# A rebuilt loading phase in a fused attention and gated feed-forward kernel on one Trainium2 core: what is loaded first, from which queue, and in what order two batches are worked through

## The chip, the cores and the metric

The kernel runs on one core of a Trainium2 chip. The metric is the time of one execution in device microseconds (us): 227.48 us, the median of three runs (227.17 to 228.03). A difference of under about 0.5% (1.14 us) can't be told from no change. The engines are named as in the profile: PE is the matmul engine (TensorE), PEld its weight loads, DVE is VectorE, ACT is ScalarE, POOL is GpSimd, SP is SyncE. SPq, POOLq and ACTq are the same engines where they issue DMAs. Each engine works through its instructions strictly in the order in which the program gives them.

## The reference

`x` is (8 batches, 8 heads, 512 tokens, 64) and `state` is (8, 8, 32, 64), both float32. Per batch and head:

```python
scores  = x @ state.T / 8            # 512 x 32
xread   = softmax(scores) @ state    # 512 x 64, the tokens read the state
scores2 = state @ x.T / 8            # 32 x 512
sread   = softmax(scores2) @ x       # 32 x 64, the state reads the tokens
attn    = concat([xread, sread])     # 544 rows per batch, heads side by side: 512 columns
# then, over all 8 * 544 = 4352 rows
out = (sigmoid(attn @ w_gate) * (attn @ w_val)) @ w_out   # 512 -> 1536 -> 512
```

## The kernel before, in words

**Tiling.** Matmul operands are bf16, sums are float32 in PSUM. For the tokens the kernel never forms `xread`: it multiplies the state with the weights first (`SW` = state times `w_gate` and `w_val`, per batch and head) and then the softmax weights `a` with `SW`. So per batch `b` the steps are, by the names of the helpers (line numbers are those of the profile):

- `load_x` (L78) brings x of a batch, 1 MB of float32, into `xf`; `cast_x` (L103) makes `xb` in bf16 from some of its heads; `xT` is its transpose, either with PE (`xT_mm` L118, copied out by `xT_cp` L123) or with four DMA transposes on SP (`at_xT_dma`, L128).
- `S_mm` (L134) makes the scores from `xT` and the zero-padded state `sTz`, `S_exp` (L139) their exponentials `E`. `n_sum` (L152, L154) sums and inverts on DVE, `n_mul` (L186) normalizes to `ab`, and `aT` is its transpose, by PE (`aT_mm` L193, `aT_cp` L203) or by DMA (`aT_dma`, L207).
- `sw_visit` and `sw_wide` make columns of `SW` from the transposed state `sTc` and the weights `wg`, `wv` (`sw_mm`, L249); `sw_cp` (L287) copies each result out of PSUM, on ACT or DVE. `sw_visit(b, lo, n, w)` needs columns lo to lo+n of weight w (0 is gate, 1 is value; without w both).
- `gv_mm` (L301) makes 128 of the 1536 hidden columns for gate and value (four 128x512 matmuls), `gv_th` (L311, ACT) a tanh in place of the sigmoid, `gv_glu` (L316, DVE) the product. `out_mm` (L332) multiplies four of twelve hidden blocks with `wo`; every third call finishes 128 rows, scales them on ACT (L336) and stores them (L338).
- `at_Eb` (L145), `p_tok` (L167 to L172), `sr_mm` (L223, L226), `sr_inv`, `sr_fin` (L231, L239) form `sread` for the state rows, which go through the feed-forward stage at the very end (L304, L352).

**Order.** The schedule is manual: the order of calls is the order of each engine's instructions. Up to the end of the `gv` work of batches 0 and 1 it is a list of calls written out by hand; after it a loop over b = 1 to 8 takes `out_mm` of batch b-1 and `gv_mm` of batch b in turn, and prepares batch b+1.

**Loads.** Weights are float32 in HBM and cast by the DMA, issued from POOL (`load_w` L83, `load_wo` L97). In the list before, SP issues the whole state `sf` (512 KB, L369), x of batch 0 in two halves and x of batch 1. POOL issues the weights one piece at a time, and between them it executes `gate` (L87): a one-element copy of something that must have landed or of a tile that is free, which holds back what POOL issues next. x of batch 1 is held by a small `memset` on POOL (`hold`, L74). The order on POOL is value columns 0 to 255, gate 0 to 255, gate 256 to 511, value 256 to 511, gate 512 to 1023, value 512 to 1023, gate 1024 to 1535, value 1024 to 1535, x of batch 2, the three thirds of `wo`, then (after the transposes of x of batch 2) x of batch 3. `pad` (L402) fills `sTz` from `sTc` on POOL; `pad(2, 6)` does batches 2 to 7.

**Warming.** `warm(n)` (L366) runs n matmuls whose result nobody reads, to keep PE busy; 80 of them before the real work.

**PSUM.** Pools named GV (2 buffers), SWP (4), OU (1) and AT (1) hold the results; a place is free again when its copy is done.

## Time and profile before

| what | value |
|---|---|
| runs: median, lowest, highest | 227.48, 227.17, 228.03 us |
| profiled execution: first to last instruction (span) | 226.7 us, granted PE clock 1.000 |
| busy PE / PEld / DVE / ACT / POOL over the span | 217.3 / 112.6 / 140.0 / 130.5 / 48.6 us |
| PE busy in 0 to 5, 5 to 10, 10 to 15, 15 to 20 us | 3.64, 3.92, 2.97, 4.97 us |
| PE busy in 20 to 40, 40 to 45, 45 to 65 us | 20.00, 4.43, 19.65 us |
| DVE and ACT busy in 15 to 45 us | 27.01 and 23.40 us |
| DMA share in 0 to 5, 5 to 10, then each 5 us to 45 | 0.64, 1.04, 1.35, 1.26, 1.13, 1.12, 1.20, 1.41, 1.19 |
| read from HBM, written to HBM | 18.35 MB, 8.91 MB |

The median is about 0.8 us above the profiled span: what lies before the first and after the last instruction, and the scatter of the runs. Busy matmul time counts pipelined matmuls, so a busy PE isn't PE at its peak. The DMA share is a mean over the core's 16 DMA engines; it passes 1 where packets of several transfers are open at once. An issue's "us to landing" runs from the issue to the last byte's arrival, so it holds the time in the queue too.

### The profile page before, as it was taken

What the parts mean: (1) busy time and instruction counts of PE and PEld (TensorE: products, weight loads), DVE (VectorE), ACT (ScalarE), POOL (GpSimd) and SP (SyncE); (2) the same over time, 40 slices, a digit from 0 to 9 for tenths busy, and PEclk for the clock granted to TensorE, in tenths of its full rate; (3) what the DMA queues carried; (4) which work ended last, traced back from release to release, by engine and by line L of the source; (5) the groups of instructions that cost most, each with busy time, mean ns of one, the idle gap of its engine ahead of it and who ended that gap; (6) DMA issues with size and microseconds to landing.
All of it is one profiled execution on the core that took longest, in us unless ns stands there. A gap on an engine that the chain in (4) does not pass through costs nothing.

```text
span 226.7 us, 4784 instructions
## 1 busy us (share of the span) xinstructions
PE 217.3 (96%) x1851; PEld 112.6 (50%) x1876; DVE 140.0 (62%) x233; ACT 130.5 (58%) x244; POOL 48.6 (21%) x96
## 2 busy tenths in 40 slices
PE   7869999999999999999999999999999999999994
PEld 7755344444444544444544444454445444466744
DVE  2579899866458855886488648874687533422311
ACT  3559788557476566746675667556765444423311
POOL 3887961016023001500060006000200000000001
PEclk9999999999999999999999999999999999999999
DMA  6999999962699444624381431234122111121114
GB/s 225 263 199 178 206 263 176 77 196 61 115 257 287 111 98 151 216 46 90 122 254 40 83 118 46 81 61 139 46 72 69 48 49 46 50 76 64 46 25 114
DMA packets 37990, 27.57 MB, mean 122 GB/s; under 512 B 20976, under 2 KB 33136, under 8 KB 37968
## 3 DMA queue, kind: packets, MB, share of 16 engines
q1 hardware_dynamic: 31408, 20.26, 35.2%
q0 software_dynamic: 6416, 6.95, 16.8%
q8 instruction: 14, 0.23, 0.4%
q14 instruction: 8, 0.07, 0.2%
q10 hardware_dynamic: 144, 0.07, 0.1%
HBM read 18.35 MB, written 8.91 MB: 120 GB/s over the span
## 4 chain that ended last, share of the span: by engine, by line
PE 77%; DMA 12%; POOL 4%; ACT 2%; SPq 2%; issue 1%; another core or an unknown queue 0%; DVE 0%; POOLq 0%
PE outp L332 36%; PE gvp L301 28%; PE gvp L304 5%; DMA xf<-in_x_dram 4%; PE swp L249 4%; DMA wg<-in_moe_w_gate_dram 3%; DMA xT<-xb 3%; SPq L128 2%; DMA sf<-in_state_dram 2%; ACT SW L287 2%; PE Sp L134 1%; PE srp L226 1%; PE outp L352 1%; POOL xb L103 1%; POOL pre L87 1%
## 5 line engine op out<-in xcount | busy, mean ns | idle before, releaser
L316 DVE SCALAR_TENSOR_TENSOR glu<-th,gvp 128x512 bf16<-128x512 f32 (+1 forms) x108 | 70.3, 657 | 62.9 <-ACT th L311 47.4
L301 PE MATMUL gvp<-aT,SW 128*128 128x512 bf16 x384 | 96.5, 380 | 0.1
L332 PE MATMUL outp<-wo,glu 128*128 128x512 bf16 x371 | 95.1, 380 | 1.2
L311 ACT ACTIVATE th<-gvp 128x512 f32<-128x512 f32 (+1 forms) x108 | 61.5, 575 | 60.1 <-PE gvp L301 49.5
L301 PEld LDWEIGHTS <-SW 128*128 128x128 bf16 x384 | 36.1, 98 | 45.4 <-issue 4.9
L332 PEld LDWEIGHTS <-glu 128*128 128x128 bf16 x396 | 37.4, 98 | 40.8 <-issue 0.4
L287 ACT CAST SW<-swp 128x512 bf16<-128x512 f32 x76 | 42.0, 590 | 5.1 <-PE swp L249 3.7
L145 POOL CAST Eb<-E 128x256 bf16<-128x256 f32 x32 | 11.7, 414 | 86.9 <-ACT E L139 86.9
L336 ACT ACTIVATE res<-outp 128x512 f32<-128x512 f32 x33 | 19.7, 598 | 17.2 <-PE outp L332 16.5
L103 POOL CAST xb<-xf 128x1024 bf16<-128x1024 f32 (+1 forms) x14 | 15.4, 1127 | 11.7 <-PE swp L249 6.1
L287 DVE CAST SW<-swp 128x512 bf16<-128x512 f32 x20 | 13.6, 684 | 2.2 <-PE swp L249 2.2
L343 POOL DMA_DIRECT2D out_dram<-res x2 | 1.0, 521 | 60.0 <-ACT res L336 60.0
L186 DVE TENSOR_TENSOR ab<-E,ri 128x512 bf16<-128x512 f32 x15 | 13.1, 878 | 0.1
L160 DVE TENSOR_REDUCE E<-E 128x128 f32<-128x512 f32 x12 | 12.4, 1037 | 0.0
L152 DVE TENSOR_REDUCE rs<-E 128x16 f32<-128x512 f32 x16 | 10.9, 680 | 2.3 <-ACT E L139 2.2
L249 PE MATMUL swp<-wg,sTc 64*32 64x256 bf16 (+1 forms) x256 | 11.5, 329 | 0.6 <-DMA wg<-in_moe_w_gate_dram 0.5
L139 ACT ACTIVATE E<-Sp 128x512 f32<-128x512 f32 x16 | 9.6, 604 | 3.6 <-PE Sp L134 3.5
L249 PEld LDWEIGHTS <-sTc 64*32 64x32 bf16 x512 | 6.2, 91 | 10.6 <-issue 7.6
L249 PE MATMUL swp<-wv,sTc 64*32 64x256 bf16 (+1 forms) x256 | 10.4, 324 | 0.0
L366 PE MATMUL warm<-ident 128*128 128x128 bf16 x80 | 7.2, 264 | 1.4 <-POOL ident masks.py:199 1.4
L231 DVE RECIPROCAL r<-srp 128x128 f32<-128x128 f32 x8 | 7.6, 950 | 1.4 <-PE srp L226 1.4
L134 PEld LDWEIGHTS <-xT 128*128 128x128 bf16 x128 | 5.7, 98 | 4.6 <-DMA xT<-xb 1.1
(60 smaller groups left out, 114.3 us busy)
## 6 DMA issues: line engine op xcount, KB each, us to landing
out_dram<-res SPq DMA_DIRECT2D x31, 256.0 KB, 2.5
xf<-in_x_dram SPq DMA_DIRECT2D x5, 1024.0 KB, 7.6
xf<-in_x_dram POOLq DMA_DIRECT2D x2, 1024.0 KB, 8.5
wo<-in_moe_w_out_dram POOLq DMA_DIRECT2D x3, 512.0 KB, 14.1
xf<-in_x_dram SPq DMA_DIRECT2D x2, 512.0 KB, 5.0
wg<-in_moe_w_gate_dram POOLq DMA_DIRECT2D x2, 512.0 KB, 8.1
wv<-in_moe_w_val_dram POOLq DMA_DIRECT2D x2, 512.0 KB, 7.2
sf<-in_state_dram SPq DMA_DIRECT2D x1, 512.0 KB, 3.5
```

The lines of the kernel that those rows point to most:

```text
L103: cp(xbs[b].rearrange("p c h d -> p h c d")[:, lo:lo + n], xfs[b][:, lo:lo + n])
L145: nc.gpsimd.tensor_copy(Ebs[b][:, c], E1s[b][:, c])
L160: nc.vector.tensor_reduce(held["E4", b][:, e].rearrange("p j n -> p (j n)"), E1s[b][:, :, e].rearrange("p c j n -> p (j n) c"), AX.X, ALU.add)
L186: eng.tensor_tensor(abs_[b].rearrange("p c e (j n) -> p (c e) j n", n=Ns)[:, :, 2 * i:2 * i + 2], halfE(b, i), ri.unsqueeze(3).to_broadcas ...
L249: nc.tensor.matmul(pss[e][j * Ns:(j + 1) * Ns, o:o + n], sTc[rows, b, j], (wg, wv)[w][rows, j, lo:lo + n], start=True, stop=True)
L287: cp(*sw_left.pop((b, lo, w, e)))
L301: nc.tensor.matmul(ps, SWs[b][:, g, w, fs], aTs[b][:, :, g], start=(g == 0), stop=(g == 1))
L304: nc.tensor.matmul(ps, (wg, wv)[w][:, j, fs], XS[:, j], start=(j == 0), stop=(j == 3))
L311: nc.scalar.activation(th, held["gv", b, f][0], AF.Tanh, scale=0.5)
L316: nc.vector.scalar_tensor_tensor(glus[b][:, f], held["th", b, f], 1.0, held["gv", b, f][1], ALU.add, ALU.mult)
L332: nc.tensor.matmul(ops[b, c], glus[b][:, f, c * 128:(c + 1) * 128], wo[:, f], start=(f == 0), stop=(f == NF - 1))
L336: nc.scalar.activation(res, ops[b, c], AF.Copy, scale=0.5)
```

## The change

The changed kernel loads the state in four pieces of two batches each. The first (128 KB) comes from ACT's queue ahead of everything on ACT. x of batch 0 comes from SP in four pieces of two heads. x of batch 1 moves from SP to POOL, as the first transfer there, and the first five weight pieces follow it with no gate between; the three other pieces of the state come from POOL after the first `at_Eb`. Gate columns 1024 to 1535 come after x of batch 2; x of batch 3 comes right after the first third of `wo`; the second third is behind the gate on the transposes of x of batch 2, and the last third behind a cast of x of batch 3 and `pad(2, 6)`. The transposed state of the first two batches is written into `sTz` by ACT straight from PSUM (`sT_pad`), the other six batches are transposed in the middle of the `gv` work. PE's transposes of x go by tiles of two heads, scores can be made for half a tile (`jjs`), and `n_mul` can take a part. The list of calls up to the end of batch 1 has a new order, with 70 warming matmuls. The loop after it is as it was. Cut to its core (the old list of calls is in the functions above, and of the unchanged bodies nothing is shown):

```diff
     vec, act, pool = nc.vector.tensor_copy, nc.scalar.copy, nc.gpsimd.tensor_copy
-    def load_x(b, eng, parts=1, hold=None):
+    def load_x(b, eng, parts=1):
         xf = stg.tile((128, H, 4, D), FP, name="xf")
-        if hold is not None:
-            hold.memset(xf[:, 0, 0, 0:1], 0.0)
         v = x[b].rearrange("h (p c) d -> p h c d", c=4)
         n = H // parts
         for i in range(parts):
...
         nc.gpsimd.tensor_copy(pre[:, 1:2], landed)
     def load_wo(q):
         nc.gpsimd.dma_start(wo[:, 4 * q:4 * q + 4],
                             moe_w_out.rearrange("(k p) n -> p k n", p=128)[:, 4 * q:4 * q + 4])
...
     held = {}
-    def xT_mm(b, i, place):
-        ps = held["xT", b, i] = place[0].tile((128, 2, 4, 128), BF, name="xTp", tag=place[1])
-        for jj in range(2):
-            for c in range(4):
-                j = 2 * i + jj
-                nc.tensor.transpose(ps[:, jj, c], xbs[b][:, c, 2 * j:2 * j + 2].rearrange("p h d -> p (h d)"), ident)
-    def xT_cp(b, i, jj, cp):
-        js = slice(0, 2) if jj is None else slice(jj, jj + 1)
-        cp(xT_tile(b)[:, 2 * i + js.start:2 * i + js.stop], held["xT", b, i][:, js])
+    def xT_mm(b, j, place):
+        ps = held["xT", b, j] = place[0].tile((128, 4, 128), BF, name="xTp", tag=place[1])
+        for c in range(4):
+            nc.tensor.transpose(ps[:, c], xbs[b][:, c, 2 * j:2 * j + 2].rearrange("p h d -> p (h d)"), ident)
+    def xT_cp(b, j, cp):
+        cp(xT_tile(b)[:, j], held["xT", b, j])
     def at_xT_dma(b):
         xT = xT_tile(b)
         for c in range(4):
             nc.sync.dma_start_transpose(xT[:, :, c], xbs[b][:, c].rearrange("p h d -> p (h d)"))
-    def S_mm(b, i, place):
-        ps = held["S", b, i] = place[0].tile((128, 4, 2, 2, Ns), FP, name="Sp", tag=place[1])
-        for jj in range(2):
+    def S_mm(b, i, place, jjs=(0, 1)):
+        if jjs[0] == 0:
+            held["S", b, i] = place[0].tile((128, 4, 2, 2, Ns), FP, name="Sp", tag=place[1])
+        ps = held["S", b, i]
+        for jj in jjs:
             for c in range(4):
                 nc.tensor.matmul(ps[:, c, :, jj], xTs[b][:, 2 * i + jj, c], sTz[:, b, 2 * i + jj], start=True, stop=True)
...
         else:
             nc.vector.tensor_tensor(Es[b][:, 1], held["E4", b], Es[b][:, 0], ALU.subtract)
-    def n_mul(b, i, eng):
+    def n_mul(b, i, eng, lo=0, n=4):
         if b not in abs_:
             abs_[b] = ap_.tile((128, 4, 2, 128), BF, name="ab")
-        ri = held["ri", b, i]
-        eng.tensor_tensor(abs_[b].rearrange("p c e (j n) -> p (c e) j n", n=Ns)[:, :, 2 * i:2 * i + 2], halfE(b, i),
-                          ri.unsqueeze(3).to_broadcast((128, 8, 2, Ns)), ALU.mult)
+        ri, ce = held["ri", b, i], slice(2 * lo, 2 * lo + 2 * n)
+        eng.tensor_tensor(abs_[b].rearrange("p c e (j n) -> p (c e) j n", n=Ns)[:, ce, 2 * i:2 * i + 2],
+                          halfE(b, i)[:, ce], ri[:, ce].unsqueeze(3).to_broadcast((128, 2 * n, 2, Ns)), ALU.mult)
     def aT_mm(b, place):
         ps = held["aT", b] = place[0].tile((128, 4, 2, 128), BF, name="aTp", tag=place[1])
...
         for _ in range(n):
             nc.tensor.matmul(ps[:, :128], ident, ident, start=True, stop=True)
-    sf = wp.tile((128, 16, D), FP, name="sf")
-    nc.sync.dma_start(sf, state.rearrange("b h (u l) d -> (b h u) l d", l=16))
-    load_x(0, nc.sync, 2)
-    wfs = {}
+    sfs, stp = {}, {}
+    def load_s(q, n, eng):
+        sfs[q] = stg.tile((128, n, 4, D), FP, name="sf", bufs=1, padded_shape=(128, 3, 4, D))
+        for i in range(n):
+            eng.dma_start(sfs[q][:, i], state[2 * (q + i):2 * (q + i) + 2].rearrange("b h (u l) d -> (b h u) l d", l=4))
+    def sT_mm(q, place, i=0):
+        ps = stp[q + i] = place[0].tile((128, 4, 64), FP, name="stp", tag=place[1])
+        for l in range(4):
+            for e in range(2):
+                nc.tensor.matmul(ps[e * 64:(e + 1) * 64, l], sbs[q][:, i, l], ident_e[:, e], start=True, stop=True)
+    def sT_cp(q, cp):
+        cp(sTc[:, 2 * q:2 * q + 2].rearrange("p b j (u l) -> p (b j u) l", u=8), stp[q].rearrange("p l g -> p g l"))
+    def sT_pad(q, e, cp):
+        rows = slice(e * 64, (e + 1) * 64)
+        cp(sTz[rows, 2 * q:2 * q + 2, :, e].rearrange("p b j (u l) -> p (b j) u l", u=8),
+           stp[q][rows].rearrange("p l (g u) -> p g u l", u=8))
+    def pad(b, n=1):
+        for e in range(2):
+            rows = slice(e * 64, (e + 1) * 64)
+            nc.gpsimd.tensor_copy(sTz[rows, b:b + n, :, e], sTc[rows, b:b + n])
+    sbs = {}
+    def cast_s(q, n, cp):
+        sbs[q] = stg.tile((128, n, 4, D), BF, name="sb", bufs=1, padded_shape=(128, 3, 4, D))
+        cp(sbs[q], sfs[q])
+    load_s(0, 1, nc.scalar)
+    load_x(0, nc.sync, 4)
     make_identity(nc, ident)
     nc.vector.memset(sTz, 0.0)
     for e in range(2):
         nc.gpsimd.memset(ones[:, e, e * 64:e * 64 + 64], 1.0)
         nc.gpsimd.memset(ones[:, e, 64 - e * 64:128 - e * 64], 0.0)
-    ident_e = ident.rearrange("p (b e u) -> p e b u", e=2, u=2)
+    ident_e = ident.rearrange("p (g e u) -> p e g u", e=2, u=8)
     pre = wp.tile((128, 2), FP, name="pre")
     nc.scalar.activation(pre[:, 0:1], ident[:, 0:1], AF.Exp)
-    warm(36, SWP)
-                nc.tensor.matmul(ps[e * 64:(e + 1) * 64, l], sb[:, 8 * i + l], ident_e[:, e], start=True, stop=True)
+    warm(8, OU)
+    warm(8, SWP)
+    cast_x(0, act, 0, 2)
+    cast_s(0, 1, vec)
+    sT_mm(0, SWP)
+    xT_mm(0, 0, AT)
+    cast_x(0, vec, 4, 2)
+    warm(14, OU)
+    xT_cp(0, 0, vec)
+    sT_pad(0, 0, act)
+    load_x(1, nc.gpsimd)
     cast_x(0, act, 2, 2)
+    load_w(0, 0, 256)
+    cast_x(0, vec, 6, 2)
+    xT_mm(0, 2, GV)
+    sT_pad(0, 1, act)
     load_w(1, 0, 256)
     load_w(0, 256, 256)
+    S_mm(0, 0, AT, (0,))
+    xT_cp(0, 2, vec)
+    xT_mm(0, 1, SWP)
+    xT_cp(0, 1, act)
+    xT_mm(0, 3, SWP)
+    warm(12, GV)
+    load_w(1, 256, 256)
+    S_mm(0, 1, OU, (0,))
+    xT_cp(0, 3, vec)
+    load_w(0, 512, 512)
+    S_mm(0, 1, OU, (1,))
+    S_exp(0, 1)
+    cast_x(1, vec, 4, 4)
+    S_mm(0, 0, AT, (1,))
+    warm(17, GV)
     S_exp(0, 0)
     n_sum(0, 0)
+    cast_x(1, pool, 0, 2)
+    xT_mm(1, 2, OU)
+    sT_cp(0, act)
     n_sum(0, 1)
+    cast_x(1, pool, 2, 2)
+    xT_cp(1, 2, act)
     n_mul(0, 1, nc.vector)
+    xT_mm(1, 3, SWP)
+    xT_cp(1, 3, act)
     xT_mm(1, 0, AT)
+    xT_mm(1, 1, GV)
+    xT_cp(1, 0, act)
+    warm(8, SWP)
+    n_mul(0, 0, nc.gpsimd)
+    at_Eb(0)
+    xT_cp(1, 1, act)
+    warm(3, SWP)
+    S_mm(1, 1, GV)
     sw_visit(1, 0, 256)
+    sw_visit(0, 0, 256)
+    aT_mm(0, AT)
+    S_exp(1, 1)
     sw_cp(1, 0, 2, 0, act)
+    sw_cp(1, 0, 2, 1, vec)
     S_mm(1, 0, GV)
+    sw_cp(0, 0, 2, 1, act)
+    sw_cp(0, 0, 2, 0, vec)
+    sr_mm(0, OU)
+    aT_cp(0, 0, vec)
+    sw_visit(0, 256, 256)
+    load_s(1, 3, nc.gpsimd)
+    aT_cp(0, 1, act)
     n_sum(1, 1)
+    n_mul(1, 1, nc.gpsimd)
     S_exp(1, 0)
+    sw_cp(0, 256, 2, 0, act)
+    n_sum(1, 0)
+    gv_mm(0, 0, SWP)
+    n_mul(1, 0, nc.vector)
+    gv_th(0, 0)
     load_w(1, 512, 512)
     gv_mm(0, 1, GV)
     sw_cp(0, 256, 2, 1, act)
     gv_glu(0, 0)
     gv_th(0, 1)
+    sw_visit(1, 256, 256)
+    load_w(1, 1024, 512)
+    load_x(2, nc.gpsimd)
+    sw_cp(1, 256, 2, 0, act)
+    p_tok(1)
+    aT_mm(1, AT)
+    gv_mm(0, 2, SWP)
+    gv_glu(0, 1)
+    sw_cp(1, 256, 2, 1, vec)
     aT_cp(1, 0, act)
+    gv_mm(0, 3, GV)
+    load_w(0, 1024, 512)
+    gv_th(0, 2)
+    cast_s(1, 3, pool)
+    gv_glu(0, 2)
+    aT_cp(1, 1, act)
     sw_visit(0, 512, 512, 0)
     gv_th(0, 3)
+    at_Eb(1)
     gv_glu(0, 3)
     sw_cp(0, 512, 0, 1, vec)
+    gv_mm(1, 1, SWP)
+    sw_cp(0, 512, 0, 0, act)
+    gv_mm(1, 0, GV)
+    gv_th(1, 1)
+    gv_mm(1, 2, SWP)
+    gv_th(1, 0)
+    gv_glu(1, 1)
+    gv_th(1, 2)
+    sw_visit(0, 512, 512, 1)
+    gv_glu(1, 0)
+    gv_mm(1, 3, GV)
+    gv_glu(1, 2)
+    sw_visit(1, 512, 512, 1)
+    sw_cp(0, 512, 1, 0, act)
+    sw_cp(0, 512, 1, 1, vec)
+    load_wo(0)
+    gv_th(1, 3)
+    sw_cp(1, 512, 1, 1, vec)
+    sT_mm(1, AT, 0)
+    sw_cp(1, 512, 1, 0, act)
+    sw_visit(1, 512, 512, 0)
+    gv_glu(1, 3)
+    sr_fin(0)
+    sw_cp(1, 512, 0, 1, act)
+    sw_cp(1, 512, 0, 0, act)
+    gv_mm(0, 4, SWP)
+    gv_th(0, 4)
     gate(xfs[0][:, 0, 0, 0:1])
+    gv_mm(0, 6, GV)
+    gv_glu(0, 4)
     gv_mm(0, 5, SWP)
+    load_x(3, nc.gpsimd)
+    gv_th(0, 6)
+    gv_glu(0, 6)
+    gv_th(0, 5)
+    gv_mm(1, 5, SWP)
+    gv_glu(0, 5)
+    gv_mm(1, 4, GV)
+    gv_th(1, 5)
+    gv_glu(1, 5)
+    gv_th(1, 4)
+    gv_mm(1, 6, SWP)
+    gv_th(1, 6)
+    sT_cp(1, act)
+    gv_glu(1, 4)
+    sw_visit(0, 1024, 512, 1)
+    cast_x(2, pool, 0, 4)
+    gv_glu(1, 6)
+    sw_cp(0, 1024, 1, 1, act)
+    gv_mm(1, 7, GV)
+    gv_th(1, 7)
+    sw_cp(0, 1024, 1, 0, act)
+    sT_mm(1, AT, 1)
+    gv_glu(1, 7)
+    sT_mm(1, OU, 2)
+    sw_visit(1, 1024, 512, 1)
+    sw_cp(1, 1024, 1, 1, vec)
+    sw_visit(0, 1024, 512, 0)
+    gv_mm(0, 7, GV)
+    sw_cp(0, 1024, 0, 1, vec)
+    sT_cp(3, act)
+    sw_cp(1, 1024, 1, 0, act)
+    sw_cp(0, 1024, 0, 0, act)
+    sr_mm(1, OU)
+    sw_visit(1, 1024, 512, 0)
+    cast_x(2, pool, 4, 4)
+    gv_th(0, 7)
+    at_xT_dma(2)
+    gate(xTs[2][:, 0, 3, 0:1])
+    gv_glu(0, 7)
+    sT_cp(2, vec)
+    sw_cp(1, 1024, 0, 1, vec)
+    sw_cp(1, 1024, 0, 0, act)
+    gv_mm(0, 8, SWP)
+    gv_mm(0, 9, GV)
+    gv_th(0, 8)
+    gv_mm(1, 9, SWP)
+    gv_glu(0, 8)
+    gv_mm(0, 10, SWP)
+    gv_th(0, 9)
+    gv_glu(0, 9)
+    gv_th(1, 9)
+    gv_mm(1, 8, GV)
+    gv_glu(1, 9)
+    gv_th(0, 10)
+    gv_glu(0, 10)
     load_wo(1)
     gv_th(1, 8)
+    cast_x(3, pool, 0, 4)
     gv_glu(1, 8)
     gv_mm(1, 11, SWP)
     gv_mm(1, 10, SWP)
+    gv_mm(0, 11, GV)
     gv_th(1, 11)
+    gv_th(0, 11)
+    sr_fin(1)
+    cast_x(3, act, 4, 4)
+    gv_glu(1, 11)
     gv_th(1, 10)
+    gv_glu(0, 11)
+    pad(2, 6)
     gv_glu(1, 10)
+    load_wo(2)
```

## The prediction

> **What bounds the kernel now.** I read the page's busy shares and slices first, then the chain of waits in order of time, the timeline up to 50 us, the waits of each engine, and the DMA issues one by one.
>
> ```profile
> PE 217.3 (96%) x1851; PEld 112.6 (50%) x1876; DVE 140.0 (62%) x233; ACT 130.5 (58%) x244; POOL 48.6 (21%) x96
> PE   7869999999999999999999999999999999999994
> POOL 3887961016023001500060006000200000000001
> ```
>
> PE is full from the third slice on (each is 5.67 us). So the change can win only what PE loses before, and at places where a later stage still waits for a load. The chain names both:
>
> ```profile
> 7.81 7.18 DMA wg<-in_moe_w_gate_dram
> ...
> 22.91 10.01 DMA xf<-in_x_dram
> 33.07 2.03 POOL xb L103 x2
> 35.12 1.29 SPq L128
> 36.45 1.26 SPq L128
> 37.76 1.30 SPq L128
> 39.10 5.76 DMA xT<-xb
> 44.91 0.55 PE Sp L134 x13
> ```
>
> Start and length in us, then what. The first real `sw` matmul waits for weights until 15.0. Later the path leaves PE: x of batch 2 (issued 22.91, landed 32.9), two POOL casts, four transposes issued by SP, the last landing at 44.9, and only then the scores of batch 2. On PE this reads:
>
> ```profile
> 18.32 1.90 PE L301 MATMUL gvp<-aT,SW 128*128 128x512 bf16 x8
> ...
> 43.75 0.40 PE L134 MATMUL Sp<-sTz,xT 128*128 128x64 bf16 x2
> 44.44 0.20 PE L134 MATMUL Sp<-sTz,xT 128*128 128x64 bf16 x1 [0.29 <-DMA xT<-xb]
> 44.91 0.55 PE L134 MATMUL Sp<-sTz,xT 128*128 128x64 bf16 x13 [0.27 <-DMA xT<-xb]
> 45.30 2.75 PE L332 MATMUL outp<-wo,glu 128*128 128x512 bf16 x11
> ```
>
> The `gv` phase of batches 0 and 1 starts at 18.3 and ends at 43.75; the scores take 1.55 instead of some 0.75 (8 of them take 0.40), and `out` starts at 45.30. From there little is idle: 4.80 to 4.95 of every 5 us. I put `out_mm(0, 4)`, the first to need the last third of `wo`, at 45.30 plus four `out` calls of 0.86 plus one `sw_wide` of 0.77: **49.5 us** now. What follows is the same code, so that point's shift is the change's gain. The profiled span is 226.7; the median, 227.48, is 0.8 above it, and I add shifts to the median.
>
> **Start of the gv phase.** Two chains race.
>
> Weights: the fourth 256-column piece landed at 17.7 (issued 10.89, 6.8 to landing), with 4.72 MB up to it (state 0.52, x 2.10, weights 2.10). After the change it is 4.33 MB. Landings from 13.7 (value piece, issued 5.43, 8.3) to 22.8 (issued 15.77, 7.0) bring 3.67 MB in 9.1 us, 0.40 MB/us; 0.39 MB less is 1.0 us. The gates' holes come on top: the DMA share is 0.64 in the first 5 us, and x of batch 1 is issued only at 4.8. I take 0.6 (0 to 1.6, the latter if x follows without a hole). So the piece lands at 16.1, its visit takes 0.34 (21.61 to 21.95), and the first `gv` is at 16.4.
>
> x of batch 1: 12.4 now, 0.39 MB less ahead, no hold: 9.4 to 10.4. Then on DVE, which works in order, a cast of four heads (0.86, twice the 0.43 of 128x512), two sums with inverses (0.94 each), a product (0.95), two `sw_cp` (0.69 each) and half of `aT` (0.42), with ACT's half and hand-overs behind it 6.2 in all: 15.6 to 16.6. I take **16.3** for the start, 2.0 earlier; bounds 15.4 to 17.3.
>
> **Moved into the gv phase.** Counted on PE: `sw_visit(1, 256, 256)`, 0.34, and 24 matmuls for six batches' state (32 took 1.06 before 6.4 us), 0.8 and three switches, 1.0. The phase grows by 1.35: end at 16.3 + 25.45 + 1.35 = **43.1**. The x transposes are as many as before, in tiles of four; two copies of half a tile take 0.42 each on DVE for one of 0.69, beside PE's wait for x. ACT gets `sT_pad`, `sT_cp` and a cast of x of batch 3 (1.05), some 2.5 us; it is busy 23.4 of the 30 us from 15 to 45, which hides that. If x of batch 3 lands after 41, that cast holds the last tanh in ACT's queue; I count on some 37. DVE is busy 27.0 of those 30 us and gets about as much as it gives; a loss there of up to 0.8 or a gain of as much stays in the range.
>
> **The front end.** ACT's DMA issue goes ahead of its 1.28 us table load; ACT has 2.06 us of idle time after that, which hides it. Four x issues on SP instead of two cost 0.4 each, with nothing behind them. POOL issues six DMAs at 0.75 to 0.93 from 1.65 on and is free at 6.5, before x of batch 1 lands; three more for the state, 2.2 in all, end where `n_mul(1, 1)` could start (16.2).
>
> The row on queues: the value piece issued on POOL at 5.43 landed at 13.7, after x of batch 1 (issued on SP at 4.8, landed 12.4), though it is half its size. The Trainium skill (DMA: Bandwidth & Descriptors, Queues, rings and completion order) says that an engine goes round the queues packet by packet. By that rule the ungated x of batch 1 would halve the rate of x of batch 0, putting the last piece some 1 us later; by the row SP's transfer goes first. x of batch 1 lands the same either way, so the sum stays.
>
> **Warming** falls from 80 to 70 matmuls.
>
> ```profile
> 1.36 4.02 PE L366 MATMUL warm<-ident 128*128 128x128 bf16 x36 [1.36 <-POOL ident masks.py:199]
> ...
> 10.40 1.50 PE L366 MATMUL warm<-ident 128*128 128x128 bf16 x24
> ```
>
> The early ones take 112 ns each, later ones 62, though the page's PEclk is 9 throughout. In 10 to 15 us PE is busy 2.97 of 5 and stays fast; the change leaves similar gaps, so I price it at nothing. The other end is one stretch of 4 us at half speed, 2 us, most of it before x lands. The skill (TensorE: Matmul & The Clock Gate, Part 1) puts the fall after an idle window of 3.4 us; by that the changed order, with no such gap that I can see, loses nothing either.
>
> **What is late next: x of batch 2, POOL's queue and `wo`.** POOL's order after the change is the gate on the transposes of batch 2, `load_wo(1)` (0.77), half a cast of batch 3 (1.0), `pad(2, 6)` (1.70), `load_wo(2)`. The scores of batch 2 need that `pad`; before it was done at 31.2, long before the transposes. So after the transposes POOL now adds 0.2 + 3.5 us ahead of the scores, and two thirds of `wo`, which landed at 38.7 and 41.7 in the old order, are asked for only then.
>
> x of batch 2 has 8.9 MB up to it instead of 10.0 (the last gate piece now follows it), 2.6 to 3.3 us by the spacing of the landings, and the start gains 0.6 to 1.6; against this `n_mul(1, 1)` keeps POOL from issuing the next weights until 17, when the queue is nearly empty: landing at 29.0 (28.0 to 30.0). From landing to the last transpose it took 12.0 now, with 3 MB of `wo` behind it. For batch 3 with nothing behind it takes 9.5: casts from 52.20, issues from 54.54 to 60.6, then 1 to 2. After the change 3 MB are behind it again (gate piece, a third of `wo`, x of batch 3), so I stay nearer to the 12.0: 11.0, the gate opens at **40.0** (37.5 to 42).
>
> Then `pad` is done at 43.7, and the scores start at 43.7 rather than 43.1. 1 MB alone from POOL took 6.9 from issue to landing (x of batch 3, issued 45.16); a 64 KB store from POOL takes 2.2, which with 2.6 for the stream bounds it from below at 4.8. I take 6.4: `load_wo(1)` lands at 46.6, where `out_mm(0, 2)` wants it at 43.7 + 0.8 + 1.7 = 46.2. The last third lands 2.6 to 3 later by the spacing, at 49.2 (gate plus 7.6 to 10.6). `out_mm(0, 4)` could go at 46.6 + 0.86 + 0.77 + 0.86 = 49.1. So it goes at **49.2 instead of 49.5**: a gain of 0.3, 227.2 us. The 2.0 us won in front shrink to 0.3 because the wait has moved behind POOL's queue.
>
> **Rivals.**
>
> - Transposes and `wo` are in time, and PE decides. For: with the gate at 38.8 or before, everything lands as PE wants it; 9.5 from landing to transposes is on record. Against: 3 MB behind. Then the scores start at 43.1, `out` at 43.85 and the point is 48.05: 1.5 less, 226.0; with the phase starting at 15.4, 225.1.
> - Slower: POOL's queue behind the gate. The gate opens at 41.6 or later (x of batch 2 at 29.6 and the full 12.0): `pad` ends at 45.3, `out` starts at 46.1, the last third of `wo` lands at 50.8 to 51.8: 1.3 to 2.3 more, 229.0. It decides above 41.4; below 40.3 it wins instead of losing.
> - The ungated queue does nothing, since the DMA share is over 1 from 5 us on and the bytes decide. The start gains only the 1.0 of the bytes, the phase ends at 44.1, and the point is 49.05 by PE, or 49.5 by `wo`: 227.0 to 227.5.
>
> **How the numbers follow.** Forecast (226.4 to 228.5) 0.33, in time 0.34, slower 0.22, nothing gained 0.11. Nearly all of the first and the last is within 0.5% (1.14 us, about what a measurement can tell from no change). So faster 0.34, same 0.44, slower 0.22. The range reaches from 225.0 (in time, early start) to 229.0. Both signs are open, and the forecast's own range is the narrower one.
>
> **What would show it.** Right: first `gv` near 16.3; the scores of batch 2 waiting for POOL's `pad` instead of a DMA; `out` on PE with gaps for `wo` at 46 to 49. Wrong: no idle time on PE from 42 to 50 (then it is faster), a first `gv` after 17.3, `sw` of columns 512 on waiting for weights, matmuls of 112 ns after 12 us, or ACT waiting for x of batch 3.

## The result, and the profile after

The changed kernel takes 235.16 us (median of four runs, 233.67 to 236.56) against 227.75 us of the kernel before (four runs, 227.17 to 229.3): a ratio of 1.031 with the interval 1.025 to 1.038. It is slower by 7.4 us, where 227.2 us and at most 229.0 had been predicted. The profiled span is 234.8 us instead of 226.7; the profiled run is the slowest of the changed kernel's four, so a difference between single spans overstates a little. Runs that fell into a slower state, at a lower clock, are left out of every ratio here.

From the page of the changed kernel, the engines' busy time and three rows of the 40 slices (5.87 us each):

```profile
PE 221.0 (94%) x1841; PEld 115.1 (49%) x1866; DVE 139.2 (59%) x235; ACT 132.4 (56%) x251; POOL 48.9 (21%) x86
PE   5399999959999999999999999999999999999994
POOL 8218981073004100420042003200200000000001
DMA  7992999966379945443744251135112111112113
```

PE has a new hole in the second slice and one in the ninth (47 to 53 us). The DMA row falls to 2 in the fourth slice, where it should be full of weights. The chain of waits of the changed kernel up to 62 us (start, length, what) names what stands behind both:

```profile
2.26 8.72 DMA xf<-in_x_dram
...
14.40 1.81 PE warm L355 x17
...
22.93 1.49 POOL wv L80 x2
24.42 9.59 DMA xf<-in_x_dram
...
34.12 2.03 POOL xb L93 x2
...
41.18 5.45 DMA xT<-xb
...
47.95 1.05 POOL xb L93
49.00 0.78 POOL sTz L383
...
49.83 0.83 POOL sTz L383
```

The last of the four pieces of x of batch 0, 256 KB, lands at 10.98; in the kernel before, the second half had landed at 7.2. x of batch 2 is issued only at 24.42, behind two value pieces that POOL issues behind a product of 1.04 us (before: 22.91), and lands at 34.0. Then the transposes, and behind the gate at 46.75 the issue of a third of `wo`, the cast of batch 3 and `pad` on POOL. The timeline of PE of the changed kernel shows what PE pays:

```profile
9.31 0.61 PE L107 MATMUL xTp<-ident,xb 128*128 128x128 bf16 x4 [2.50 <-DVE xb L93]
...
14.21 2.00 PE L355 MATMUL warm<-ident 128*128 128x128 bf16 x17
...
21.46 1.89 PE L290 MATMUL gvp<-aT,SW 128*128 128x512 bf16 x8
...
41.22 7.08 PE L290 MATMUL gvp<-aT,SW 128*128 128x512 bf16 x32
50.70 0.63 PE L123 MATMUL Sp<-sTz,xT 128*128 128x64 bf16 x16 [2.40 <-POOL sTz L383]
51.17 4.44 PE L321 MATMUL outp<-wo,glu 128*128 128x512 bf16 x11
```

And the windows of the changed kernel (window, busy PE, PEld, DVE, ACT, POOL with counts; then granted clock, DMA share, GB/s):

```profile
15.00:20.00 5.00, 5.00 (x97) 4.74 (x95) 3.46 (x7) 3.87 (x9) 3.53 (x7) 1.00 0.53 89
50.00:55.00 5.00, 4.25 (x26) 1.90 (x27) 3.62 (x7) 1.09 (x2) 3.23 (x6) 0.68 1.09 175
```

In the kernel before, the last `gv` matmuls of the phase are these:

```profile
36.83 7.08 PE L301 MATMUL gvp<-aT,SW 128*128 128x512 bf16 x32
```

The point that the prediction followed, `out_mm(0, 4)`, moved from 49.6 to 57.2 (the second group of `out` starts at 56.31 instead of 48.76, and the point is one call of 0.86 later). The 7.55 us are four terms:

- the first `gv` comes at 21.46 instead of 18.32 (+3.14);
- the `gv` phase is 26.84 long (21.46 to 48.30) instead of 25.59 (18.32 to 43.91, where the last `gv` ends): +1.25. The prediction's 25.45 ends at 43.75, where the first scores start;
- from the end of the phase to the first `out` it is 2.87 instead of 1.39 (+1.48);
- the first twelve `out` matmuls take 4.37, from 51.17 to the next `sw`, instead of 2.69 (+1.68), at a granted clock of 0.68 in 50 to 55.

Behind that point another 0.5 us of the 8.1 between the spans is lost.

### The profile page after: what moved, and what is told of

It reads as the page before. It is cut to its first block, busy times and chain, and to the rows that moved or that the text cites. A ratio compares the mean times of both kernels' runs of the same rounds, so it can differ in the third digit from the quotient of the medians.

```text
span 234.8 us, 4775 instructions
## 1 busy us (share of the span) xinstructions
PE 221.0 (94%) x1841; PEld 115.1 (49%) x1866; DVE 139.2 (59%) x235; ACT 132.4 (56%) x251; POOL 48.9 (21%) x86
## 3 DMA queue, kind: packets, MB, share of 16 engines
q1 hardware_dynamic: 30256, 18.69, 31.7%
## 4 chain that ended last, share of the span: by engine, by line
PE 78%; DMA 10%; POOL 3%; SPq 3%; DVE 2%; issue 1%; ACT 1%; another core or an unknown queue 0%; POOLq 0%; DVEq 0%
PE outp L321 35%; PE gvp L290 27%; DMA xf<-in_x_dram 8%; PE gvp L293 5%; PE swp L238 4%; DMA xT<-xb 2%; SPq L115 2%; PE Sp L123 2%; PE warm L355 2%; POOL xb L93 1%; PE srp L215 1%; PE outp L341 1%; ACT SW L276 1%; PE xTp L107 1%; POOL sTz L383 1%
## 5 line engine op out<-in xcount | busy, mean ns | idle before, releaser
L321 PE MATMUL outp<-wo,glu 128*128 128x512 bf16 x371 | 96.8, 385 | 1.2
L300 ACT ACTIVATE th<-gvp 128x512 f32<-128x512 f32 (+1 forms) x108 | 62.2, 576 | 60.5 <-PE gvp L290 49.9
L134 POOL CAST Eb<-E 128x256 bf16<-128x256 f32 x32 | 12.4, 428 | 99.6 <-ACT E L128 99.6
L325 ACT ACTIVATE res<-outp 128x512 f32<-128x512 f32 x33 | 19.7, 598 | 17.2 <-PE outp L321 16.5
L276 DVE CAST SW<-swp 128x512 bf16<-128x512 f32 x21 | 14.2, 685 | 5.0 <-PE swp L238 5.0
L93 POOL CAST xb<-xf 128x1024 bf16<-128x1024 f32 (+1 forms) x13 | 14.2, 1115 | 4.6 <-DMA xf<-in_x_dram 4.6
L175 DVE TENSOR_TENSOR ab<-E,ri 128x512 bf16<-128x512 f32 x14 | 11.5, 823 | 0.1
L238 PE MATMUL swp<-wv,sTc 64*32 64x256 bf16 (+1 forms) x256 | 10.3, 324 | 0.0
L355 PE MATMUL warm<-ident 128*128 128x128 bf16 x70 | 7.9, 298 | 1.4 <-POOL ident masks.py:199 1.4
L123 PE MATMUL Sp<-sTz,xT 128*128 128x64 bf16 x128 | 6.7, 199 | 2.4 <-POOL sTz L383 2.4
```

What stands on the lines that cost most here:

```text
L93: cp(xbs[b].rearrange("p c h d -> p h c d")[:, lo:lo + n], xfs[b][:, lo:lo + n])
L123: nc.tensor.matmul(ps[:, c, :, jj], xTs[b][:, 2 * i + jj, c], sTz[:, b, 2 * i + jj], start=True, stop=True)
L134: nc.gpsimd.tensor_copy(Ebs[b][:, c], E1s[b][:, c])
L238: nc.tensor.matmul(pss[e][j * Ns:(j + 1) * Ns, o:o + n], sTc[rows, b, j], (wg, wv)[w][rows, j, lo:lo + n], start=True, stop=True)
L276: cp(*sw_left.pop((b, lo, w, e)))
L300: nc.scalar.activation(th, held["gv", b, f][0], AF.Tanh, scale=0.5)
```

## The experiments

Each edit is shown against the kernel that it starts from. Spans are those of the profiled runs.

### Why does the first `gv` come at 21.46?

**x of batch 1 from SP**, into the changed kernel:

```diff
-    load_x(1, nc.gpsimd)
+    load_x(1, nc.sync)
```

> The changed kernel with one word changed: x of batch 1 is issued by SP behind the four pieces of x of batch 0, not as POOL's first transfer. Theory A (a transfer on POOL's queue takes most of the DMA engines' time from what SP has queued, so the last pieces of batch 0 are starved): the last piece, which landed at 10.98 us, lands before 7.5; the first gv matmul comes at 18.0 to 19.5 instead of 21.5; the time falls by 2 to 4 us, to 231 to 233. Rival B (four pieces of 256 KB are slow as such, from one queue or the other): the last piece still lands after 10, the first gv stays within 0.7 of 21.5 and the time within 1 us of 235.

Measured: ratio 1.035 (1.027 to 1.043), span 235.3. The last piece of batch 0 landed at 9.1, not before 7.5, x of batch 1 only at 15.2, and the first `gv` came at 22.34. So it is not x of batch 1 alone that takes the rate from SP's queue: the weights behind it in POOL's queue do it too, though less, and with x of batch 1 on SP they delay that instead. How much each queue moved from 5 to 9 us stands in the two profiles (packets, MB, share of 16 engines; q0 carries POOL's transfers, q1 SP's). First the changed kernel, then this run:

```profile
q0 software_dynamic: 325, 0.99, 79.5%
q1 hardware_dynamic: 206, 0.20, 16.4%
...
q1 hardware_dynamic: 518, 0.51, 45.2%
q0 software_dynamic: 637, 0.32, 65.7%
```

With x of batch 1 in POOL's queue (packets of 3.0 KB in the mean, SP's 1.0 KB) SP moved a sixth of the bytes; with weights there (0.5 KB) it moved the larger part. The shares go with the size of POOL's packets here; that the size is the reason was not tested by itself.

**x of batch 1 held until batch 0 has landed**, into the changed kernel:

```diff
+    gate(xfs[0][:, 6, 0, 0:1])
     load_x(1, nc.gpsimd)
```

> The changed kernel with one gate put back: POOL waits for the last piece of x of batch 0 before it issues x of batch 1 and the weights behind it. Theory A (starved by POOL's queue): the last piece lands before 7, x of batch 1 at 11 to 13 instead of 10.3, the fourth 256-column piece at 17.5 to 19 instead of 16.0; the first gv at 19 to 20; the time falls by 1 to 2.5 us. Rival B (the small pieces are slow as such): the last piece still lands after 10, everything behind the gate is later still, first gv after 24, and the time rises by over 2 us.

Measured: ratio 1.028 (1.020 to 1.036), span 233.9. The last piece landed at 6.7, so 4.3 us of its lateness were the neighbours in the other queue, and small pieces on SP are not slow by themselves. But x of batch 1 then lands at 13.4, PE waits 3.21 us for its cast and its granted clock falls (0.80 in 10 to 15, 0.52 in 15 to 20), and the first `gv` comes at 21.19: the wait has moved to the next transfer.

**The kernel before with only x of batch 1 moved to POOL, ungated:**

```diff
+    load_x(1, nc.gpsimd)
     pre = wp.tile((128, 2), FP, name="pre")
...
-    load_x(1, nc.sync, 1, nc.gpsimd)
```

> The kernel before with x of batch 1 issued as POOL's first transfer, without its hold; SP issues the state and the two halves of x of batch 0 as before, and the weights keep their gates. Theory A (what POOL queues takes most of the DMA engines' time from SP's queue): the second half of x of batch 0, which landed at about 7.2, lands at 9 to 11, although x of batch 1 lands earlier than 12.4; the first score matmul comes 1.5 us later or more, the first gv later than 18.3, and the time rises by 0.5 to 3 us. Rival M (an earlier x of batch 1 is worth more than a late half of batch 0): the first gv comes at or before 17.8 and the time falls.

Measured: ratio 1.013 (1.005 to 1.021), span 229.5. One transfer in the other queue makes the second half of batch 0 land at 11.2 instead of 7.2. PE's timeline of this kernel, at the first transposes that need it and at the first `gv`:

```profile
11.86 1.03 PE L118 MATMUL xTp<-ident,xb 128*128 128x128 bf16 x8 [3.90 <-ACT xb L103]
...
21.93 1.90 PE L301 MATMUL gvp<-aT,SW 128*128 128x512 bf16 x8
```

That alone delays the first `gv` by 3.6 us; the whole change delays it by 3.14. Part of the 3.6 is PE's clock: after its wait of 3.90 us the granted clock is 0.50 in 10 to 15 and 0.82 in 15 to 20.

**x of batch 1 straight behind batch 0 on SP, the weights held until batch 0 has landed**, into the changed kernel:

```diff
-    load_x(1, nc.gpsimd)
+    load_x(1, nc.sync)
     cast_x(0, act, 2, 2)
+    gate(xfs[0][:, 6, 0, 0:1])
     load_w(0, 0, 256)
```

> The changed kernel with only the front mended (x of batch 1 from SP, one gate before POOL's first weights). The last piece of batch 0 lands before 7, x of batch 1 at 10 to 11, the first gv comes at 16.8 to 18. But POOL's order behind it is unchanged, so that x of batch 2 is issued at about 20, the gate opens at 42 to 43.5 and the scores wait for pad until 46 or 47 after an idle PE: the loss against before is still 2.5 to 4.5 us. Rival: with the start mended the late chain no longer counts, and the time is within 1.2 us of before.

Measured: ratio 1.012 (1.004 to 1.020), span 231.3. The last piece of batch 0 landed at 7.6 and the first `gv` came at 18.20, both a little later than expected. This edit alone takes back the larger part of the loss, from 1.031 to 1.012, in intervals that do not overlap; but the start is hardly earlier than the 18.32 of the kernel before. The timeline of PE of this kernel shows the next load that is late:

```profile
18.20 1.90 PE L290 MATMUL gvp<-aT,SW 128*128 128x512 bf16 x8
...
27.29 0.41 PE L238 MATMUL swp<-wv,sTc 64*32 64x512 bf16 x8 [1.53 <-DMA wv<-in_moe_w_val_dram]
```

Value 512 to 1023 is issued at 19.36, behind POOL's casts and products. Later the scores wait 1.58 us for `pad`, with the gate at 44.11.

**Warming groups taken out** of the changed kernel (they stand in its chain with 1.28 and 1.81 us):

```diff
-    warm(12, GV)
...
-    warm(17, GV)
...
-    warm(8, SWP)
...
-    warm(3, SWP)
```

> The changed kernel without its four later groups of warming matmuls (12, 17, 8 and 3); the 30 before them stay. Theory E (with the data late and PE on its slow clock, the groups of 12 and 17 stand in the chain with 1.3 and 1.8 us): the first gv comes 2 to 3 us earlier, at 18.5 to 19.5, and the time falls by 1 to 3 us even if the first matmuls of the gv phase run slow. Rival F (the groups only fill waits, or they keep PE fast): the first gv stays within 0.7 of 21.5, or comes earlier but the matmuls from there run at half speed for several us, and the time stays or rises.

Measured: ratio 1.031 (1.022 to 1.040), span 234.1. The first `gv` is 1.2 earlier (20.24), less than expected, and not all of that can be put down to the groups: in two runs below that change nothing ahead of it (`pad` ahead of the gate, 44 warming matmuls) it comes at 21.25 and 20.60. The time is the same: the scores then wait 2.83 us for `pad`, since the gate still opens at 46.05. What is won ahead of the gate is lost at it.

### Why do the scores and `out` come late?

**The loads behind POOL's work moved up** in the changed kernel:

```diff
     load_w(0, 512, 512)
+    load_w(1, 512, 512)
+    load_w(1, 1024, 512)
+    load_x(2, nc.gpsimd)
...
-    load_w(1, 512, 512)
...
-    load_w(1, 1024, 512)
-    load_x(2, nc.gpsimd)
```

> The changed kernel with three POOL loads (value columns 512 to 1023 and 1024 to 1535, x of batch 2) moved up to stand directly behind the first five weight pieces. Theory C (the empty DMA queue between 17 and 25 us, because these issues stand behind at_Eb and n_mul in POOL's order, makes x of batch 2 late, and with it the gate, pad and the scores of batch 2): x of batch 2 lands before 29 instead of 34.0, the last transpose of batch 2 before 42 instead of 46.6, the scores start without waiting for pad at about 48.3 instead of 50.7, out runs at full clock, and the time falls by 2.5 to 3.5 us, to about 232. Rival D (the wait behind the gate is set by the transposes or by POOL's work, whenever x of batch 2 lands): the scores still start after 50 and the time stays within 1 us of 235.

Measured: ratio 1.022 (1.015 to 1.030), span 231.9. x of batch 2 lands at 27.0 for 34.0, but POOL comes to its casts only at 32.1. The gate opens at 43.7 for 46.75, the scores (48.32) no longer wait, and the first twelve `out` matmuls take 2.71. The span is 2.9 shorter, but 1.0 of that stands already at the first `gv` (20.43), which this edit does not aim at. By the ratios the gain is 0.9%, some 2 us, and the intervals of the two kernels overlap. So the place of these loads in POOL's order sets the wait at the gate; what it costs is some 2 us.

**`pad` ahead of the gate** in the changed kernel:

```diff
+    pad(2, 6)
     gate(xTs[2][:, 0, 3, 0:1])
...
-    pad(2, 6)
```

> The changed kernel with pad(2, 6) moved on POOL from behind the gate on the transposes of batch 2 (and behind a third of wo and a cast) to ahead of that gate; the two thirds of wo stay behind it. Theory G (POOL's 3.7 us behind the gate delay the scores of batch 2, and with an idle PE its clock falls): the scores start at 48.3 without a wait instead of 50.7, the next 12 out matmuls run at 0.22 us each instead of 0.35, and the time falls by 1 to 2 us, the rest being taken back by wo, which still lands 5.7 us after its issue behind the gate at some 47. Rival H (the scores wait for the transposes themselves, and out for wo): the scores stay after 50, or out stalls on wo until 57 as now, and the time stays within 0.7 us.

Measured: ratio 1.030 (1.023 to 1.038), span 233.5. The scores start at 47.87 without a wait, 2.8 earlier. From PE's timeline of this kernel:

```profile
51.75 1.02 PE L321 MATMUL outp<-wo,glu 128*128 128x512 bf16 x4 [1.50 <-DMA wo<-in_moe_w_out_dram]
...
55.90 1.89 PE L321 MATMUL outp<-wo,glu 128*128 128x512 bf16 x8 [1.38 <-DMA wo<-in_moe_w_out_dram]
```

The two thirds of `wo` behind the gate take `pad`'s place. In the changed kernel that wait was hidden by `pad`'s. The ratio stays as it was.

**`pad` behind the gate in the kernel before:**

```diff
-    pad(2, 6)
     cast_x(2, pool, 0, 4)
...
     gate(xTs[2][:, 0, 3, 0:1])
+    pad(2, 6)
     load_x(3, nc.gpsimd)
```

> The kernel before with pad(2, 6) moved on POOL behind the gate on the transposes of batch 2; everything else as before. Theory G (a pad behind the gate is on PE's path): the scores of batch 2 start 1.9 us after the last transpose, at 46.9 instead of 44.9, and if PE's 3 us of idle time cost it the fast clock, out needs 1.5 more: 2 to 3.5 us slower than before, 229.5 to 231. Rival (pad is hidden behind the end of the gv phase): within 0.7 us of before.

Measured: ratio 1.005 (1.000 to 1.010), span 226.8, not the loss of 2 to 3.5 us that I had expected. In this profile the gate opened at 43.06 and the scores came at 44.94, after 1.02 us for `pad`, where they had waited for the transposes before. The gate was 1.9 us earlier than in the kernel before (44.92), with x of batch 2 landing 1.0 earlier; that is why `pad` cost so little here. That work behind the gate is dear only when the gate is late follows from this arithmetic; no run shows `pad` behind a gate at 44.92.

**44 warming matmuls behind the last `gv`** of the changed kernel:

```diff
     gv_mm(0, 11, GV)
+    warm(44, AT)
     gv_th(1, 11)
```

> The changed kernel with 44 warming matmuls (some 2.5 us) behind the last gv matmul of batch 1, where PE idles 2.4 us. Theory K (PE loses its fast clock in that idle time): the scores still start at about 50.7, but the 12 out matmuls from there take 2.7 us instead of 4.4, the granted clock between 50 and 55 is 1.00 instead of 0.68, and the time falls by 1.3 to 1.8 us. Rival L (these matmuls are slow because of what they read, or because DMAs and casts run beside them): they still take over 4, and the time stays within 0.5 us of the changed kernel.

Measured: ratio 1.026 (1.017 to 1.034), span 232.7. The scores come at 50.05; PE's timeline of this kernel:

```profile
47.28 2.62 PE L355 MATMUL warm<-ident 128*128 128x128 bf16 x44
50.05 0.63 PE L123 MATMUL Sp<-sTz,xT 128*128 128x64 bf16 x16
50.51 2.75 PE L321 MATMUL outp<-wo,glu 128*128 128x512 bf16 x12
```

The idle time was filled, and the twelve matmuls take 2.7 instead of 4.4 at a granted clock of 1.00. So the term of 1.7 us is the clock. The time as a whole shows it less clearly: the median is 0.6 us lower, the ratio 0.6%, with intervals that overlap, and in this profile the first `gv` was 0.9 earlier besides.

**The last third of `wo` behind the gate in the kernel before:**

```diff
-    load_wo(2)
...
     gate(xTs[2][:, 0, 3, 0:1])
+    load_wo(2)
     load_x(3, nc.gpsimd)
```

> The kernel before with one load moved: the last third of wo is issued behind the gate on the transposes of batch 2, ahead of x of batch 3. Theory N (the transposes of batch 2 are slow because three thirds of wo are in the queue with them; 12.0 us from x's landing to the last transpose against 9.5 without them): they end 1 to 2 us earlier, the scores start without their wait, out at 44.6 instead of 45.3, and the last third still lands before 49.5: 0.3 to 0.8 us faster than before. Rival O (the last third is late there as it is in the changed kernel, or the transposes are slow by themselves): out stalls on wo, or nothing changes: same or up to 1 us slower.

Measured: ratio 0.998 (0.993 to 1.003), span 226.7. From landing (31.7) to the gate (41.12) the casts and transposes took 9.4 us for 12.0, and the scores wait for nothing; no difference in time can be told, in a profile whose first `gv` was 0.8 later (19.12).

### Is that all?

**The late part**: the loads up as above, the casts and transposes of batch 2 ahead of the cast of the state, `pad` ahead of the gate, and the thirds of `wo` earlier:

```diff
+    cast_x(2, pool, 0, 4)
+    cast_x(2, pool, 4, 4)
+    at_xT_dma(2)
     cast_s(1, 3, pool)
...
     load_wo(0)
+    load_wo(1)
...
     load_x(3, nc.gpsimd)
+    load_wo(2)
```

> The changed kernel with only the late part mended (as in the run of both parts); the front as in the changed kernel. The first gv stays at 20.4 to 21.5, the scores start at 47.3 to 48.4 without a wait and out neither stalls on wo nor runs slow: 3 us are left of the loss against before (2 to 4), the late part being worth 3.5 to 4.5. Rival: the late loss comes from the late start alone, and mending POOL's order gives under 1.5 us.

Measured: ratio 1.022 (1.015 to 1.029), span 232.2. First `gv` at 20.79; the scores (48.68) and `out` (49.15) wait for nothing. But by the ratio 5 us of the loss are left, where 2 to 4 were expected: the late part is worth some 2 us, no more than the loads moved up by themselves. In this run and in that one PE also waits 1.30 us for DVE's product `ab` inside the `gv` phase, which it does in neither of the two kernels compared.

**The late part with the mended front:**

> The changed kernel with its front and its late part mended, the new order of the calls otherwise kept. Front: SP issues x of batch 1 behind batch 0, POOL's weights wait by one gate for the last piece of batch 0. Late: three loads up, casts and transposes of batch 2 ahead of cast_s, the second third of wo behind the first and the last behind x of batch 3, pad ahead of the gate. If the four causes found are all there is (starved pieces of batch 0, an empty queue from 17 to 25, POOL's work and wo behind the gate, the slow clock after an idle PE), the first gv comes at 17 to 18, the scores start at 44 to 45 without a wait, and the time is within 1.2 us of the kernel before, on either side. If something else in the new order costs time, it stays 2 us or more above before.

Measured: ratio 1.021 (1.015 to 1.027), span 231.7, far from the expected. The three loads that were moved up keep POOL issuing until 13.7, so its casts of batch 1, landed at 10, come late: PE idles 2.69 us at 14.41, its clock falls to 0.66, and the first `gv` comes at 20.27. The moved issues delayed POOL's own work as the change had delayed SP's transfers.

**The front mended, the loads behind POOL's first product**, `sr_mm(0, OU)` behind the first `gv` call, the other state pieces behind `n_mul(1, 1)`; the casts and transposes of batch 2 ahead of the first third of `wo`, the second third behind it, `pad` ahead of the gate and the last third behind it:

```diff
     n_mul(0, 0, nc.gpsimd)
+    load_w(1, 512, 512)
+    load_w(1, 1024, 512)
+    load_x(2, nc.gpsimd)
     at_Eb(0)
...
     n_mul(1, 1, nc.gpsimd)
+    load_s(1, 3, nc.gpsimd)
```

> The changed kernel with its front mended as in e12_front_part (x of batch 1 from SP, the weights on POOL behind a gate on the last piece of batch 0), and with POOL's queue mended without delaying its casts of batch 1: value 512 to 1023, value 1024 to 1535 and x of batch 2 are issued behind POOL's half of the normalization of batch 0, ahead of at_Eb(0); sr_mm(0) moves behind the first gv call, the other state pieces behind POOL's n_mul(1, 1); the casts and transposes of batch 2 come ahead of the first third of wo, pad ahead of the gate, the second third before and the last third directly behind it. Theory (the loss is front, POOL's order and what stands behind the gate, each mended here): first gv at 18.2 (17.9 to 18.8), no wait of over 0.3 us for value 512 to 1023, x of batch 2 landed by 28 to 30, the scores of batch 2 straight behind the gv work at 45.0 to 45.6, out at 45.5 to 46.1, against 45.30 in the kernel before; time 227.5 to 228.6, ratio 0.999 to 1.004. The 1.4 us of work that the change moved into the gv phase then stay as its only cost, and they eat what the earlier start could win. Rival (something else in the new order of calls costs time on PE, ACT or DVE between 18 and 45 us): the same first gv, but the gv phase longer than 27.1 us without a wait for a load, or gaps on PE that end on ACT or DVE, and a ratio over 1.008.

Measured: ratio 1.036 (1.029 to 1.043), span 234.5. First `gv` at 17.16, but the state pieces, issued behind x of batch 2, landed at 28.8 and held POOL's cast, and PE with it. PE's timeline of this kernel:

```profile
29.82 0.32 PE L369 MATMUL stp<-ident,sb 128*64 128x64 bf16 x8 [2.54 <-POOL sb L389]
```

Then x of batch 3 and two thirds of `wo` ran beside the transposes, the last of which landed at 49.1. The ratio is over the rival's 1.008, but the gaps end on loads and on POOL's cast of a late load, not on ACT or DVE: they are two new mistakes in POOL's queue, and the run decides nothing between theory and rival.

**The mended front, nearly the old order on POOL, the new list on the other engines:**

```diff
     n_mul(0, 0, nc.gpsimd)
+    load_w(1, 512, 512)
+    load_s(1, 3, nc.gpsimd)
+    load_w(1, 1024, 512)
+    load_x(2, nc.gpsimd)
...
     n_mul(1, 1, nc.gpsimd)
+    at_Eb(0)
...
     load_w(0, 1024, 512)
+    load_wo(0)
+    load_wo(1)
...
     gate(xTs[2][:, 0, 3, 0:1])
+    load_wo(2)
...
+    pad(2, 6)
+    load_x(3, nc.gpsimd)
```

> The front of e12_front_part and, behind POOL's half of the normalization of batch 0, about the order that POOL had in the kernel before: value 512 to 1023, the three other state pieces, value 1024 to 1535, x of batch 2, n_mul(1, 1), at_Eb(0), p_tok(1), gate 1024 to 1535, two thirds of wo, the casts of the state and of batch 2 with its transposes, then the gate, the last third of wo, pad, x of batch 3 and its whole cast on POOL. In e13_front_and_pool the state pieces had gone behind x of batch 2 and landed at 28.8; POOL's cast of them held PE for 2.5 us, and x of batch 3 and two thirds of wo ran beside the transposes, which ended at 49.1; here both are ahead. Theory (the new list of calls costs only its moved work, 1.4 us, when the loads come in time): first gv at 17.2 to 18.4, gv phase of 26.6 to 27.2 us without a wait of over 0.5 us for a load, its end at 44 to 45.5, x of batch 2 landed by 28 to 30, transposes by 39 to 41, out at 45 to 46.5 (before: 45.30), time 227.0 to 229.0, ratio 0.997 to 1.006. Rival (the new list costs more than that whatever the loads do): gaps on PE between 18 and 45 us that end on ACT, DVE or POOL's own work and not on a load, out after 47, ratio over 1.01.

Measured: span 227.9, ratio 1.013 (1.005 to 1.021), from runs that lie 3 us apart (229.64 to 232.83). PE's timeline of this kernel:

```profile
17.23 0.30 PE L238 MATMUL swp<-wv,sTc 64*32 64x256 bf16 x8 [1.00 <-DMA wv<-in_moe_w_val_dram]
17.47 1.90 PE L290 MATMUL gvp<-aT,SW 128*128 128x512 bf16 x8
...
38.11 7.08 PE L290 MATMUL gvp<-aT,SW 128*128 128x512 bf16 x32
45.03 0.63 PE L123 MATMUL Sp<-sTz,xT 128*128 128x64 bf16 x16
45.49 2.78 PE L321 MATMUL outp<-wo,glu 128*128 128x512 bf16 x12
```

From the first `gv` to the scores PE waits for nothing. The phase is 27.7 long (17.47 to 45.19); 0.9 of that is `sr_mm(0)`, which I had moved into it, so the moved work is 1.2, as in the changed kernel. `out_mm(0, 4)` comes at 49.84: of the 7.55 us 0.2 are left. That is what the theory said for this stretch, and the rival, a list that costs more by itself, has no gap to show there.

The time does not bear the theory out. Its ratio of 1.013 is above the 0.997 to 1.006 that the theory gave and above the 1.01 that the rival asked for; only the lower end of the interval reaches the theory. The profile is of the fastest of these runs. In it 1.2 us of span are left, 0.3 of them in a wait for ACT's `res` at 65.8; what the other runs, up to 3 us longer, lose is in no profile. So up to `out_mm(0, 4)` the loss is accounted for, and whether the new list costs something behind it stays open. No kernel that I tried is faster than the kernel before.

## Why the prediction was wrong

**The step that failed first: "by the row SP's transfer goes first", and with it "x of batch 1 lands the same either way, so the sum stays".** The prediction had one row (a 512 KB piece from POOL, issued at 5.43, landing after the 1 MB that SP had issued at 4.8) and chose it over round-robin. But that row shows a transfer from POOL that starts when SP's queue is already full, not two queues that start together. Here POOL's transfer took the larger part: its 1 MB, issued at 1.59, landed at 10.3, ahead of SP's last 256 KB, issued at 2.26 and landed at 10.98, and from 5 to 9 us POOL's queue moved 0.99 MB and SP's 0.20.

The Trainium skill (DMA: Bandwidth & Descriptors, Queues, rings and completion order) says that an engine goes round the queues packet by packet. The landings agree in direction with that, but the delay was 3.8 us, four times the 1 us that I had worked out from it: I had taken halves, and the bytes went about five to one.

The second quotation was the error behind it. x of batch 1 did land at 10.3, inside the 9.4 to 10.4, and the fourth weight piece at 15.9 for 16.1. But the sum had two chains, and x of batch 0 was a third. On DVE, which works in order, its casts at 8.82 and 11.01 stand ahead of batch 1's. I had named its lateness and gave it no place on the path. The first `gv` came 5.2 us after the 16.3 predicted. The kernel before with that transfer alone moved shows a delay of 3.6. The whole 5.2 is not the queue's: with the front mended the first `gv` still comes 0.9 to 1.9 after 16.3.

**"`n_mul(1, 1)` keeps POOL from issuing the next weights until 17."** The mechanism was right, the size wrong: the late first data moved `n_mul(1, 1)` itself to 21.89, so x of batch 2 was issued at 24.42, the DMA share fell to 0.53 and 0.42 in 15 to 25, and it landed at 34.0, not 29.0. From landing to the last transpose it took 12.6, not 11.0. The gate opened at 46.75 instead of 40.0, well past the 41.4 above which the slower rival was to decide. That rival had the right mechanism with 2.3 us at most, since it let the gate open only a little later than the forecast did.

**"So I price it at nothing"**, of the clock. Behind the gate a wait of 2.40 us was followed by a granted clock of 0.68 in 50 to 55: 1.7 us, as filling the gap shows. The run with the loads behind POOL's first product has the same once more (2.54 us idle ahead of 29.82, then 0.66 in 30 to 35, and 24 `gv` matmuls in 7.04 us for 5.34). But the length of the gap alone does not decide: in that same run a wait of 2.87 us ahead of 56.95 left the clock at 1.00. The Trainium skill (TensorE: Matmul & The Clock Gate, Part 1) puts the fall after an idle window of 3.4 us; here shorter gaps were enough, twice, and the measurement decides.

In front PE was slow in a place that the prediction had not priced. The 16 warming matmuls at 1.36 and the 14 at 5.11 take 118 and 121 ns each, the 17 at 14.21 still 118, those at 17.71 then 71: PE had not become fast before 17.7, where the kernel before, with 36 warming matmuls in one stretch, had by 6.5. On the chain from 11.87 to 17.88 two warming groups and 16 transposes take 1.28, 1.81 and 1.66; at the 62 ns of the kernel before, and its 1.07 for 16 transposes, they would take 1.9 us less (an estimate). How much of the late start is this and how much the late data is not separated, and no run puts the early warming back.

**Slips in the sum.** The PE row of the kernel before is full from the fourth slice on, not the third, which reads 6. The slower rival's 1.3 to 2.3 us more reach 229.8, not 229.0. And the last third of `wo` stands 3.5 us behind the second on POOL, so it should have landed 3.5 later, not 2.6 to 3; it landed 3.3 later. None of the three decided the outcome.

**What held.** The phase grew by 1.25, predicted 1.35. The scores wait for POOL's `pad` instead of a DMA, at gate plus 3.9, predicted 3.7. `wo` would have been late next, as `pad` ahead of the gate shows; its two thirds behind the gate took 5.7 and 5.6 from issue to landing, where I took 6.4. ACT never waited for x of batch 3. The 2.0 us that the front was to win do not show: with the front mended the first `gv` comes at 17.2 to 18.2, when it waits for weights or has just done so, and the 1.2 us of moved work eat what is left.

## What to carry to other kernels

Give every transfer that the first work needs its own landing time under the new queues, in the order in which the in-order engine behind it will use them; the slowest of them is the start, and the transfers that were let go early compete with it. An instruction that issues a transfer is a DMA and also a place in an engine's order: ask both what the queue does to it and what its engine must do first. A wait that a late stage can hide costs nothing, as `pad` behind the gate nearly did in the kernel before (gate at 43.06, ratio 1.005); in the changed kernel, with the gate at 46.75, PE idled 2.40 us for it and lost 1.7 us to the clock on top.

## What the runs showed of the hardware

A transfer from POOL that starts beside SP's does not share evenly: 1 MB from POOL delayed the landing of 512 KB on SP from 7.2 to 11.2 us, and in the changed kernel POOL's queue moved 0.99 MB from 5 to 9 us while SP's moved 0.20. With nine transfers issued from POOL in a row, the ninth waited for the first to land, at 10.9; from POOL's timeline of the kernel with the loads moved up:

```profile
11.18 0.96 POOL L75 DMA_DIRECT2D xf<-in_x_dram  x1 [3.29 <-DMA xf<-in_x_dram]
```

In the trace the ninth reports its landing on the same semaphore as the first, so the wait can be the program's own; a limit of the hardware is not shown.

And a granted clock of 1.00 in a window need not be a measurement: in the changed kernel it reads 1.00 from 10 to 15 and from 15 to 20 us, though the 17 warming matmuls at 14.21 took 118 ns each and the 11 at 17.71 took 71. The trace holds no clock record of that kernel before 17.7 us (of the kernel before none before 6.5), and a stretch without a record reads as 1.00.
